# Blocks of v with 48 rows in place of 40 in an attention and feed-forward kernel

## The chip, the cores and the metric

The kernel runs on one core of one Trainium2 chip. The metric is the device time of one execution in microseconds, the median of several runs. The profile shows one further execution.

## What is computed

Three parts follow each other. First comes attention over 4 batches, 8 heads, 576 positions of 64 numbers, the sum of a coarse attention (q, k and v averaged over groups of four positions, its result repeated four times) and a local one, in which a position sees the seven positions around it. Then two feed-forward blocks work on the 2304 tokens of 512 numbers.

```python
out_d = sm_attn(q_d, k_d, v_d)                     # groups of four averaged
mask = np.abs(pos[:, None] - pos[None, :]) < 4
out_local = softmax(where(mask, scale * q @ k.T, -1e9)) @ v
x = (np.repeat(out_d, 4, axis=2) + out_local)      # 2304 tokens x 512
x = ((x @ w1) * (x @ w2) @ w3) @ w_out
h = x @ w_in
return (h * (1 / (1 + np.exp(-h)))) @ moe2_w_out
```

Inputs are drawn in 64-bit floats; the kernel loads q, k and v in 32 bits, and the weights as pairs of 32-bit words that VectorE and ScalarE turn into 32-bit floats. ("dec", "w_w", "st" and "lent" in the rows are tiles of this work.)

## The kernel before, in words

**Units.** Attention is cut into 16 units, each one batch and one pair of heads; one head of the pair takes partitions 0 to 63, the other 64 to 127. The names in the order list end in the unit's number: `sd`, `md`, `xd`, `rd`, `nd` are scores, maximum, exponentials and normalization of the coarse part, `s`, `mk`, `ml`, `x`, `rl`, `n` those of the local part, `td`, `cd`, `tl`, `cl` the transposes of the two sets of weights and ScalarE's copies of them, `od` and `ol` the products with v, `xf`, `xh`, `xo` their sum and its two halves for products in reduced precision.

**What a unit loads.** `Lq` (`load_qk`, L294) loads q and k, 128 rows of 4,632 bytes. `Lr` (`load_vr`, L307) loads v in groups of four, 80 rows of 4,096 bytes, for the pooled v (`pv0`, `pv1`; L478 and L485). `Lva` and `Lvb` (`load_vw`, L299) load v in blocks: for each window of 32 queries the 38 keys that it can see are laid out as 38 rows, with two rows of zeros to 40. `Lva` brings the even windows to partitions 0 to 39 (5,120 bytes a row), `Lvb` the odd windows to partitions 64 to 103 (two pieces of 2,048 bytes a row). The products of `ol` (`local_sums`, L504, matmuls on L516) read the 38 rows alone. The tile of the blocks, "vw", has one buffer: a unit's blocks are loaded when `ol` of the unit before is done. The tile of vr has one buffer too, freed by `pv1`. The arrays are laid out on the host in `kernel()`, outside the metric.

**Order.** The opening, up to the first products of x, is written out by hand as one list of names (`OPENING`): each name issues its instructions on their engines, and every engine runs its part in the order of the list. In it TensorE multiplies w3 with w_out (names `p...`, L628, tile "wp"), so that h @ w_out needs one product less later, while the first units' attention and the preparation of the weights go on in between; then the products of x with w1 and w2 begin (`ab...`, L668). The list has this order around the first loads:

```
Lwt000 Lwt001 Lwt002 Lq0 Lwo00 Lwo01 Lwt010 Lwt011 at00a d2t00a Lwo10 d1t00a Lwo11 at00b d3t00a
d2t00b d1t00b d3t00b Lva0 at00c d2t00c d1t00c d3t00c Lvb0 s0 pq0 Lr0 ao0a d2o0a sd0 z0 z1 mk0
ml0 Lq1 ...
```

After the opening a table (`SUMS`, `TURN`) says after how many steps of the products of x each unit's parts come; unit 15's products with v are done at some 304 us. What follows is feed-forward work in three stages (L1113, L1165, L1300), to the end.

**DMA.** SP alone issues DMAs. The issue of a load waits for what the tile's former users still do and for an earlier DMA, and SP works in order: a load that waits holds every DMA behind it. The opening's loads of weights (L228), of q and k (L296), of the blocks (L303) and of vr (L309) share this one queue.

Of the kernel before, what the change touches and what calls it, by code (L numbers as in the profile page):

```python
# [73 lines left out]
def tile_model(ctx: ExitStack, tc: tile.TileContext, qk, vw, vr, w12, w3t, wo, wb, out):  # L74
# [213 lines left out]
    A = {}  # L288
# [10 lines left out]
    def load_vw(u, par):  # L299
        if par == 0:  # L300
            A["vw", u] = att.tile([P, 2, 5, P], F32, tag="vw", name=f"vw{u}", bufs=1)
        n = 5 - par
        nc.sync.dma_start(  # L303
            A["vw", u][64 * par:64 * par + 40, :, :n, :], vw[u // 4, u % 4, par, :, :, :n, :]
        )

    def load_vr(u):  # L307
# [17 lines left out]
    def unit_ops(u):  # L325
# [249 lines left out]
        op("Lq" + U, lambda: load_qk(u))  # L575
        op("Lr" + U, lambda: load_vr(u))
        op("Lva" + U, lambda: load_vw(u, 0))
        op("Lvb" + U, lambda: load_vw(u, 1))
        op("pq" + U, lambda: pool_qk(u))

# [936 lines left out]
```

## Time and profile before

| | us |
|---|---|
| median of 3 runs | 808.66 |
| lowest and highest of them | 806.63, 809.44 |
| the profiled execution: its time | 808.23 |
| its span, first to last instruction | 806.4 |
| TensorE busy in the span | 791.4 (98%) |
| VectorE busy | 564.6 (70%) |
| ScalarE busy | 446.3 (55%) |
| GpSimd busy | 69.2 (9%) |

The rows further down are read like this. PE is TensorE, PEld its weight loads, DVE VectorE, ACT ScalarE, POOL GpSimd, SPq the queue of SP, which issues the DMAs. L303 is a line of the kernel. "vw<-vw" is a tile or array written from another; where both sides have one name, the left one is the tile on the chip. Times count from the start of the span. [...] A row of a wait names who waited, for whom, how long in total, how often, and the longest. A row of the chain has start, duration and what; a DMA there lasts from its issue to its landing. A row of a timeline has start, duration, engine, line, operation and count; in SP's it is the time of the issue, not of the transfer.

### The profile page before, as it was taken

How to read it: one execution, taken by the hardware profiler on the slowest of the kernel's cores; microseconds unless marked ns; L12 is line 12 of the kernel's file. 1: busy time of each engine (PE TensorE's matmuls, PEld its weight loads, DVE VectorE, ACT ScalarE, POOL GpSimd, SP SyncE). 2: the span in 40 equal slices, each digit the busy share in tenths (PEclk: the TensorE clock that was granted, in tenths of full speed). 3: DMA queues.
4: the chain of work that ended last, by engine and by line, in shares of the span. 5: the costliest groups of instructions: out<-in, count | busy, mean ns of one | idle time of the engine just before them, and what ended most of it. 6: DMA issues, size and time to landing. Idle time of an engine off the chain costs nothing.

```text
span 806.4 us, 19049 instructions
## 1 busy us (share of the span) xinstructions
PE 791.4 (98%) x7510; PEld 738.0 (92%) x7510; DVE 564.6 (70%) x870; ACT 446.3 (55%) x1136; POOL 69.2 (9%) x84
## 2 busy tenths in 40 slices
PE   9899999999999999999999999999999999999998
PEld 5455599889999999999999999999999999999998
DVE  7888885687698763746889567445466698777771
ACT  6588764745465452525457477547478545444441
POOL 3000100443243220000000000000000000000000
PEclk9999999999999999999999999999999999999999
DMA  9977864798898977225475553343887987777740
GB/s 301 365 230 224 261 204 139 238 295 280 269 306 278 297 248 246 51 51 229 154 296 174 194 182 118 137 148 112 235 263 239 287 207 184 193 191 185 194 133 27
DMA packets 132265, 168.68 MB, mean 209 GB/s; under 512 B 20176, under 2 KB 109776, under 8 KB 131792
## 3 DMA queue, kind: packets, MB, share of 16 engines
q1 hardware_dynamic: 132176, 167.46, 66.5%
q8 instruction: 59, 0.97, 0.5%
q14 instruction: 30, 0.25, 0.1%
HBM read 115.00 MB, written 52.43 MB: 208 GB/s over the span
## 4 chain that ended last, share of the span: by engine, by line
PE 85%; DMA 7%; DVE 3%; ACT 2%; SPq 1%; issue 1%; POOL 1%; DVEq 0%; ACTq 0%; POOLq 0%
PE ab L668 24%; PE yb L1113 11%; PE hx L1165 9%; PE ox L1300 8%; PE hy L1165 6%; PE oy L1300 5%; PE wp L628 4%; PE hv L1165 3%; PE hz L1165 3%; PE oz L1300 3%; PE ov L1300 2%; PE ol L516 2%; DMA A<-gd 2%; DMA qk<-qk 2%; PE od L494 1%; PE s L409 1%
## 5 line engine op out<-in xcount | busy, mean ns | idle before, releaser
L668 PE MATMUL ab<-x,w_wB 128*128 128x320 f32 (+1 forms) x768 | 108.9, 298 | 1.3 <-POOL x L546 0.9
L668 PE MATMUL ab<-x,w_wA 128*128 128x320 f32 (+1 forms) x768 | 107.0, 296 | 0.0
L668 PEld LDWEIGHTS ab<-x,w_wB 128*128 128x128 f32 x768 | 102.5, 188 | 2.9 <-issue 1.3
L668 PEld LDWEIGHTS ab<-x,w_wA 128*128 128x128 f32 x768 | 101.9, 188 | 0.5
L1113 PE MATMUL yb<-co,wy 128*128 128x384 f32 x504 | 87.5, 334 | 0.0
L1113 PEld LDWEIGHTS yb<-co,wy 128*128 128x128 f32 x504 | 87.3, 188 | 0.0
L1165 PE MATMUL hx<-yc,wc 128*128 128x384 f32 x432 | 83.0, 335 | 1.0 <-ACT u L1179 1.0
L1165 PEld LDWEIGHTS hx<-yc,wc 128*128 128x128 f32 x432 | 75.6, 188 | 1.3 <-ACT u L1179 1.3
L628 PE MATMUL wp<-w_wo,w_w 128*128 128x512 f32 x128 | 60.1, 602 | 0.2 <-DVE w_wo L198 0.2
L680 ACT COPY af<-ab 128x320 f32<-128x320 f32 (+1 forms) x64 | 25.4, 397 | 58.4 <-PE ab L668 55.8
L1165 PE MATMUL hy<-yc,wc 128*128 128x384 f32 x288 | 57.7, 335 | 0.0
L1300 PE MATMUL oy<-wo,S 128*128 128x256 f32 x432 | 54.8, 283 | 0.1
L1300 PE MATMUL ox<-wo,S 128*128 128x256 f32 x432 | 53.7, 280 | 0.4 <-ACT u2o L1313 0.4
L1300 PEld LDWEIGHTS oy<-wo,S 128*128 128x128 f32 x432 | 53.1, 192 | 0.3 <-ACT p5o L1311 0.3
L1300 PEld LDWEIGHTS ox<-wo,S 128*128 128x128 f32 x432 | 51.9, 190 | 0.7 <-ACT u2o L1313 0.6
L1149 ACT ACTIVATE c<-c 128x384 f32<-128x384 f32 x96 | 48.1, 525 | 5.9 <-DVE c L1079 5.0
L1165 PEld LDWEIGHTS hy<-yc,wc 128*128 128x128 f32 x288 | 50.7, 188 | 0.0
L686 DVE TENSOR_TENSOR cf<-ab,af 128x320 f32<-128x320 f32 (+1 forms) x64 | 28.9, 451 | 25.8 <-PE ab L668 10.9
L334 ACT ACTIVATE band<-band,sml 128x38 f32<-128x38 f32 x144 | 45.0, 321 | 2.1 <-DVE sml L425 2.1
L628 PEld LDWEIGHTS wp<-w_wo,w_w 128*128 128x128 f32 x128 | 22.4, 190 | 21.1 <-issue 18.7
L1171 ACT COPY p<-hx 128x384 f32<-128x384 f32 x24 | 11.5, 481 | 43.6 <-PE hx L1165 43.6
L980 DVE TENSOR_TENSOR co<-cb,co 128x768 fp32r<-128x768 f32 x32 | 29.3, 955 | 8.8 <-ACT co L979 8.1
(183 smaller groups left out, 1451.3 us busy)
## 6 DMA issues: line engine op xcount, KB each, us to landing
gd<-c SPq DMA_DIRECT2D x96, 192.0 KB
sw<-wb SPq DMA_DIRECT2D x32, 512.0 KB
qk<-qk SPq DMA_DIRECT2D x16, 579.0 KB
big<-gd SPq DMA_DIRECT2D x18, 512.0 KB
A<-gd SPq DMA_DIRECT2D x18, 512.0 KB
S<-gd SPq DMA_DIRECT2D x17, 512.0 KB
cb<-cd SPq DMA_DIRECT2D x10, 768.0 KB
st<-w SPq DMA_DIRECT2D x14, 512.0 KB
```

Source lines behind the costliest of these rows:

```text
L334: nc.scalar.activation(E[:, j, :], src[j], AF.Exp, bias=z[:, j:j + 1], scale=scale, accum_out=z[:, NQB + j:NQB + j + 1],)
L516: nc.tensor.matmul(acc[h][r, c0:c0 + QW], lhsT=v[k, sub, c, r], rhs=ET[k, c, q0:q0 + QW], start=True, stop=True,)
L628: nc.tensor.matmul(wp_ps[half, j], lhsT=w3v[:, k, j * P:(j + 1) * P], rhs=wov[:, k, :], start=(gp == 0 and k == 0), stop=(gp == 3 and k == 1),
L668: nc.tensor.matmul(acc[:, :N], lhsT=wv[:, i, w, kk, :], rhs=X[b, h, kk][:, j, :], start=(n == 0), stop=(n == 11),)
L680: mark(nc.scalar.copy(af, C.pop(("ab", b, h, m, 0))[:, :N]))
L686: nc.vector.tensor_tensor(out=cf, in0=C.pop(("ab", b, h, m, 1))[:, :N], in1=C.pop(("af", b, h, m)), op=ALU.mult)
L980: nc.vector.tensor_tensor(out=d[:, 1], in0=src, in1=d[:, 0].bitcast(F32), op=ALU.subtract)
L1113: nc.tensor.matmul(acc[e], lhsT=WY[o][:, a, 2 * g + k, c0:c0 + P], rhs=y[:, b, k, :], start=(n < 2 and (a, b) == (0, 0) and i in (0, 1, 2, ...
L1149: nc.scalar.activation(v, v, AF.Silu)
L1165: nc.tensor.matmul(acc, lhsT=WC[s][:, a, c, kt * P:(kt + 1) * P], rhs=y[:, b, kt, :], start=(n == 0 and i in (0, 1, 2, 4)), stop=(n == 5), ...
L1171: nc.scalar.copy(p1, X_)
L1300: nc.tensor.matmul(acc, lhsT=A[:, a, p * P:(p + 1) * P], rhs=B_[name, p // 4][:, b, p % 4, :], start=(p == 0 and q == 0 and name in begin) ...
```

## The change

Blocks of v are laid out with 48 rows, 38 of values and ten of zeros, and all 48 are loaded, to partitions 0 to 47 and 64 to 111. A load that ran on 10 DMA engines (four rows each) now runs on 16 (three rows each). The bytes of the two blocks of a unit go from 200 and 160 KB to 240 and 192. The products read the same 38 rows. No instruction is added, taken away or moved on any engine.

```diff
@@ load_vw
         n = 5 - par
         nc.sync.dma_start(
-            A["vw", u][64 * par:64 * par + 40, :, :n, :], vw[u // 4, u % 4, par, :, :, :n, :]
+            A["vw", u][64 * par:64 * par + 48, :, :n, :], vw[u // 4, u % 4, par, :, :, :n, :]
         )
@@ kernel
-    vw = np.zeros((B, H // 2, 2, 40, 2, 5, 2 * D), v.dtype)
+    vw = np.zeros((B, H // 2, 2, 48, 2, 5, 2 * D), v.dtype)
```

## Rows read from the trace of the kernel before

**Rows 1.** Busy time by stretch, around the opening and after it.

```profile
23.70:93.00 69.30, 69.22 (x888) 37.60 (x888) 60.08 (x105) 53.10 (x194) 0.00 (x0) 0.98 0.81 258
132.00:178.00 46.00, 43.31 (x794) 39.51 (x793) 34.40 (x77) 27.34 (x119) 19.68 (x19) 1.00 0.76 235
178.00:806.40 628.40, 622.39 (x5407) 615.05 (x5397) 424.41 (x613) 327.63 (x706) 39.26 (x42) 1.00 0.64 198
```

**Rows 2.** Waits of TensorE over the whole span.

```profile
PE s L409 <- DMA qk<-qk: 3.6, 1, 3.6
...
PE ab L668 <- POOL x L546: 0.9, 1, 0.9
...
PE tl L464 <- ACT ET L471: 0.6, 1, 0.6
...
PE tl L464 <- ACT EdT L453: 0.2, 1, 0.2
```

**Rows 3.** The chain that ended last, four pieces of its first 100 us.

```profile
3.08 7.68 DMA lent<-wo
...
10.78 12.84 DMA qk<-qk
...
72.57 7.76 DMA vr<-vr
...
95.47 0.29 PE tl L464
```

**Rows 4.** Timeline of SP's queue: the loads of unit 0's v, then qk1.

```profile
6.51 2.70 SPq L303 DMA_DIRECT2D vw<-vw  x2
9.49 0.33 SPq L309 DMA_DIRECT2D vr<-vr  x1
10.78 0.35 SPq L296 DMA_DIRECT2D qk<-qk  x1
```

**Rows 5.** Timeline of SP's queue in five short windows, 18.9 to 24 us.

```profile
19.05 0.33 SPq L228 DMA_DIRECT2D st<-w3t  x1
...
20.00 0.33 SPq L228 DMA_DIRECT2D st<-w3t  x1
...
21.47 0.33 SPq L228 DMA_DIRECT2D lent<-wo  x1
...
22.46 0.33 SPq L228 DMA_DIRECT2D lent<-wo  x1
...
23.64 0.33 SPq L228 DMA_DIRECT2D lent<-w3t  x1
```

**Rows 6.** Waits of SP's queue, 20.1 to 21.6 us.

```profile
SPq L228 <- DMA vw<-vw: 1.7, 2, 1.1
```

**Rows 7.** Busy time by stretch, before and during the loads of unit 0's v.

```profile
5.00:13.00 8.00, 7.38 (x102) 5.00 (x101) 7.79 (x17) 3.99 (x15) 2.53 (x7) 1.00 1.01 404
15.00:20.50 5.50, 5.09 (x17) 2.27 (x15) 3.21 (x7) 5.50 (x19) 0.00 (x0) 1.00 1.04 243
```

**Rows 8.** Timeline of SP's queue: the blocks of unit 3.

```profile
69.67 1.14 SPq L303 DMA_DIRECT2D vw<-vw  x2
```

**Rows 9.** Waits of VectorE, 62 to 96 us.

```profile
DVE vr L478 <- DMA vr<-vr: 1.1, 1, 1.1
DVE md L390 <- PE sd L380: 0.6, 1, 0.6
```

**Rows 10.** Busy time and granted clock, 24 to 28 us.

```profile
24.00:28.00 4.00, 4.00 (x81) 2.93 (x69) 3.40 (x4) 1.00 (x3) 0.00 (x0) 0.57 1.02 409
```

**Rows 11.** Timeline of TensorE: pooled scores of two units.

```profile
25.67 1.71 PE L380 MATMUL sd<-qkd 64*64 64x144 f32 x12
...
32.77 0.95 PE L380 MATMUL sd<-qkd 64*64 64x144 f32 x12
```

**Rows 12.** Busy time and DMA share while unit 2's first block is in transit.

```profile
57.30:57.80 0.50, 0.50 (x3) 0.22 (x2) 0.47 (x3) 0.50 (x1) 0.00 (x0) 1.00 0.53 215
```

## Prediction, made before the changed kernel was run

> **What bounds the kernel now.** I read the busy times by stretch first, then who waited for whom on TensorE, then the chain that ended last, and only then the DMA views of the places these point at. TensorE works 69.22 of the 69.30 us between 23.7 and 93, and all but 6 of the 628.4 us after 178 [rows 1]: it is the bound, and a faster load can only shorten one of its idle times. Its waits are few [rows 2]. The longest, 3.6 us, is for a load, that of q and k of unit 1 (qk1); 0.6 and 0.2 us go to transposes that wait for ScalarE, 0.9 to GpSimd. Between 132 and 178 it idles 2.7 us [rows 1], and no wait for a load is among them. So whatever the change gives must come ahead of 99 us, and is carried to the end from there.
>
> The chain says how the opening hangs together [rows 3]. Up to 23.62 us it is DMA alone: a load of wo issued at 3.08 lands at 10.76, which lets SP issue qk1 at 10.78, and that lands 12.84 us later and starts the local scores of unit 1. Then it is TensorE up to 61.9 us, VectorE up to 72.5, the load of vr of unit 3 (vr3) from 72.57 to 80.33, VectorE again, a weight load, ScalarE, and at 95.47 TensorE.
>
> **Where the blocks of v stand in it.** Each unit loads two, 40 rows of 5,120 and of 4,096 bytes: 200 and 160 KB. Those of unit 0 are issued from 6.51 us on (one merged row), then vr0 at 9.49 and qk1 at 10.78 [rows 4]. Eight DMAs are in flight: counted in SP's timeline, the issue at 10.78 is the eighth after that at 3.08 whose landing releases it, and so it goes on. Later issue times therefore tell the landings: SP issues at 19.05, 20.00, 21.47, 22.46 and 23.64 [rows 5], eight places after the second load of wo, the two blocks, vr0 and qk1, and the waits of 20.1 to 21.6 us are put down to vw [rows 6]. The pair costs 21.47 - 19.05 = **2.42 us** on the way to TensorE's longest wait. The stream is slow just there: 404 GB/s between 5 and 13 us, 243 between 15 and 20.5, both times with the DMA engines counted as fully busy [rows 7].
>
> **The change, part by part.**
> *The rows.* 40 rows over 10 engines are 4 rows an engine, 48 over 16 are 3. An engine that has part in the pair carries 27.6 KB in place of 36.9, a quarter less, and the six that had no part carry as much. A load has landed when its last engine is done; each landing above follows the one before, the two blocks among them, so I take the last engine to be one of the ten. Its pair: 0.75 x 2.42 = 1.82 us, **0.60 us less**. The ends: if the time goes by bytes moved and not by engines, it is 1.2 x 2.42 = 2.90, 0.48 us more. If the slow stretch comes from the uneven split alone, it lost 5.5 x (404 - 243) = 886 KB, 2.2 us at 404 GB/s, less 0.18 us for the 72 KB added: 2.0 us gained. I take 0.60: it is nearest to the issue times, which are read on this very path, while the other end would need the slow packets to have no other cause.
>
> *What that is worth.* qk1 lands 0.6 us earlier, and TensorE's 3.6 us shrink to 3.0. The later loads of the stream stand behind the same pair and move as much. TensorE then works without a gap up to 93 us, and waits 0.2 and 0.6 us for ScalarE, the second time at 95.47 [rows 2, 3]: that is what is late next. The chain that ends there began with TensorE's pooled scores, for which VectorE waited [rows 9], so the 0.6 us pass through it too.
>
> *Units 1, 2 and 4.* No wait of TensorE for their loads shows [rows 2]; in 23.7 to 93 it idles 0.08 us. I cost them at nothing: the cover is the product of w3 and wo that runs without a gap. Without it each pair would again give up to 0.6 us.
>
> *Unit 3.* Its pair is issued at 69.67 [rows 8], ahead of vr3 at 72.57, and vr3 is what VectorE waits 1.1 us for [rows 9]. A quarter of this pair is at most the 0.60 us above; at the full 404 GB/s, 25.2 an engine, 36.9 KB take 1.46 us, a quarter 0.37. I take 0.4, since fewer loads stand in this queue. It passes by VectorE and a weight load to ScalarE, and so into the 0.8 us that TensorE waits there, which also caps it.
>
> *Later pairs.* From unit 5 on they lie beside a TensorE that waits for no load [rows 2]: nothing. Their added bytes are 11 x 72 = 792 KB, 2.0 us of the stream at 404 GB/s, over some 180 us in which TensorE has its operands. Were that cover gone, each pair would cost 0.18 us.
>
> *Issue.* Two blocks issued together take SP 1.14 us [rows 8], where a load of 80 rows takes 0.33 and one of 128 rows 0.35 [rows 4]: the row count hardly counts. At worst a fifth is added, 0.2 us a pair, behind which SP waits for landings anyway. Rows 40 to 47 of each half are written and read by no product; instructions, order and waits of all engines stay the same.
>
> **The sum**, against the profiled execution's 808.23 us: -0.60 for qk1, -0.40 for vr3, 807.23. That execution lies 0.43 under the median of the runs shown, 808.66, so the forecast is **807.7 us**. A measurement of this kernel tells about 0.3%, 2.4 us, from no change (the three runs span 806.63 to 809.44), so I expect a gain too small to be told.
>
> [...] The row: the blocks move at 243 GB/s with every engine counted busy, 0.60 of the rate before [rows 7]. [...]
>
> **Rivals.**
> 1. *Slower: the blocks' time goes by their bytes.* [...] For it: the 243 GB/s at full share. Against: the last engine runs its pair when most are past theirs, so its own rows hold it. Price: +0.48 us on qk1 and +0.48 on vr3, 808.66 + 0.96 = **809.6 us**. It decides from the point at which the last engine's pair takes over 2.42 us.
> 2. *No change.* Another engine lands qk1 hardly earlier, or VectorE's work on the weights holds TensorE before 62 us, so that the 0.6 us turn into a wait there. For it: VectorE is busy 60.08 of those 69.30 us [rows 1]. Time: **808.7 us**.
> 3. *Faster: the clock stays up.* [...] The loss is 4.0 x 0.43 = 1.7 us. [...] Against it: 3.0 us are not much shorter than 3.6.
> 4. *The loads still go to ten engines.* Then each carries 4.8 rows and the pair takes 1.2 x 2.42 us: rival 1's time, 809.6. Against it: while one block alone is in transit the sixteen engines' share is 0.53 [rows 12], near ten sixteenths, so the number of engines does follow the rows, and 48 can be divided by 16.
>
> **How the numbers follow.** Chances: forecast 0.50, rival 1 0.18, rival 2 0.17, rival 3 0.12, rival 4 0.03. The range takes in rivals 3 and 1 with 0.3 us of scatter at either end: 805.7 to 809.9. What is left out, the gain of the whole 2.0 us together with the clock, or several pairs exposed at once, has under 0.2. Faster by over 0.3% means under 806.2: over half of rival 3 and some of the forecast's own scatter, 0.16. Slower by over 0.3% means over 811.1, which needs five exposed pairs at 0.48 us or causes I do not see: 0.07. Within: 0.77.
>
> **What would show it.** Right: the spacing of SP's issues that wait for the two blocks falls from 2.42 to about 1.8 us, TensorE's wait for qk from 3.6 to about 3.0, VectorE's for vr3 from 1.1 to about 0.7, and TensorE's transposes of 95.47 come near 94.5. Wrong: a spacing of 2.4 us or more (rivals 1 and 4); a shorter wait for qk with new waits of TensorE before 62 us (rival 2); a granted clock of 1.00 all through 24 to 28 us (rival 3). A time that moves with all these unchanged would mean that I read the wrong stretch.

## The result, and the profile after

The changed kernel took **812.53 us** (median of 20 runs, 807.40 to 818.71), the kernel before, beside it, 807.74 (20 runs, 804.08 to 813.17). The ratio is **1.0062, 95% interval 1.0043 to 1.0080**: slower by some 5 us, where 807.7 was forecast. The profiled execution of the changed kernel took 813.38 us, with a span of 811.6.

The first view shows how much work TensorE had in long stretches. In its rows, as in [rows 1, 7, 10, 12], stand the bounds, the length, the busy time of PE, PEld, DVE, ACT and POOL with the number of instructions, the clock granted to TensorE as a share of full speed, the mean busy share of the sixteen DMA engines, and the GB/s that they moved. The kernel before:

```profile
0.00:178.00 178.00, 169.00 (x2122) 122.92 (x2123) 140.18 (x258) 118.72 (x430) 29.90 (x42) 0.99 0.79 250
...
178.00:290.00 112.00, 111.63 (x1769) 106.07 (x1760) 87.26 (x183) 61.62 (x258) 35.98 (x39) 1.00 0.89 291
```

The changed kernel, with the stretches of [rows 1, 7] as well:

```profile
15.00:20.50 5.50, 5.49 (x18) 2.43 (x16) 3.34 (x8) 4.97 (x19) 0.00 (x0) 1.00 1.05 179
...
23.70:93.00 69.30, 68.15 (x886) 37.71 (x887) 60.05 (x105) 52.92 (x192) 0.00 (x0) 0.98 0.88 269
132.00:178.00 46.00, 41.82 (x735) 38.12 (x735) 34.91 (x74) 26.68 (x117) 19.06 (x18) 1.00 0.74 218
...
0.00:178.00 178.00, 165.73 (x2060) 120.85 (x2061) 139.86 (x255) 118.31 (x428) 29.53 (x41) 0.99 0.81 249
...
178.00:290.00 112.00, 109.84 (x1715) 103.78 (x1714) 86.21 (x181) 61.02 (x256) 34.39 (x37) 1.00 0.90 294
```

TensorE is busy 3.27 us less by 178 us and 1.79 us less from there to 290: 5.06 of the 5.2 us by which this span is longer. The stream at the blocks of unit 0 moves 179 GB/s in place of 243 [rows 7], the engines' share being full in both (1.05 and 1.04), and TensorE is no longer without a gap from 23.7 to 93 us.

TensorE's waits over the span, after:

```profile
PE s L409 <- DMA qk<-qk: 4.4, 2, 3.7
PE ol L516 <- ACT Ed L334: 2.2, 2, 1.6
PE ab L668 <- issue: 2.1, 1, 2.1
...
PE ab L668 <- POOL x L546: 1.2, 1, 1.2
...
PE tl L464 <- ACT ET L471: 0.3, 1, 0.3
```

Beside [rows 2], the wait for qk1 went from 3.6 to 3.7 us (the longest of its row; the other 0.7 us is a wait for q and k of unit 0, at 8 us); the transposes' waits shrank from 0.6 and 0.2 to 0.3; two waits are new in size, for ScalarE's weights `Ed` and one that the view puts down to nothing ("issue"). Here they stand in the timeline of TensorE, after:

```profile
55.96 1.25 PE L516 MATMUL ol<-ET,vw 38*64 38x32 f32 x68 [0.65 <-DVE vr L478]
...
95.92 0.29 PE L464 MATMUL tl<-ident,band 128*38 128x128 f32 x1 [0.30 <-ACT ET L471]
...
155.43 1.25 PE L516 MATMUL ol<-ET,vw 38*64 38x32 f32 x68 [1.64 <-ACT Ed L334]
...
289.75 2.32 PE L668 MATMUL ab<-x,w_wB 128*128 128x256 f32 x18 [2.10 <-issue]
```

Two of them go back to loads. In the chain that ended last the vr of unit 1 (issued at 41.28) stands behind the first, and behind that at 155.43 a load of weights (tile sw) that lands at 148.55; VectorE decodes it, and is late with the maxima on which ScalarE's `Ed` depends. The chain, after, with vr3 in the second row, which was issued 2.05 us later than before and landed 1.1 us later (81.41 for 80.33 us [rows 3]):

```profile
41.28 13.88 DMA vr<-vr
...
74.62 6.79 DMA vr<-vr
...
139.74 8.81 DMA sw<-wb
```

How long VectorE waited for that load is the clearest row of the later loss. Before, 136 to 156 us:

```profile
DVE sw L192 <- DMA sw<-wb: 1.3, 1, 1.3
```

After, the same stretch, with the two waits of 62 to 96 us that answer to [rows 9]:

```profile
DVE sw L192 <- DMA sw<-wb: 4.0, 1, 4.0
...
DVE vr L478 <- DMA vr<-vr: 1.4, 1, 1.4
DVE md L390 <- PE sd L380: 1.0, 1, 1.0
```

Put side by side product by product, TensorE in this execution is 0.5 us late at 23.7, 1.4 at 55.8, 0.5 again at 95.5 and 0.2 at 143.9; it loses 2.1 us between there and 154 and 1.7 at 287. So in this execution the opening's loss was largely taken up again, and most of what stayed came from 143 us on, where the prediction costed nothing.

### The profile page after: what moved, and what is told of

Its sections match the earlier page's. It is cut to its first block, busy times and chain, and to the rows that moved or that the text cites. A ratio compares the mean times of both kernels' runs of the same rounds, so it can differ in the third digit from the quotient of the medians.

```text
span 811.6 us, 19049 instructions
## 1 busy us (share of the span) xinstructions
PE 791.2 (97%) x7510; PEld 738.2 (91%) x7510; DVE 565.2 (70%) x870; ACT 446.7 (55%) x1136; POOL 69.1 (9%) x84
## 4 chain that ended last, share of the span: by engine, by line
PE 82%; DMA 11%; DVE 3%; ACT 1%; issue 1%; SPq 1%; POOL 1%; DVEq 0%; ACTq 0%; POOLq 0%
PE ab L668 23%; PE yb L1113 11%; PE hx L1165 9%; PE ox L1300 8%; PE hy L1165 6%; PE oy L1300 5%; PE hv L1165 3%; PE hz L1165 3%; PE oz L1300 3%; DMA vr<-vr 3%; PE ov L1300 2%; DMA A<-gd 2%; PE ol L516 2%; DMA qk<-qk 2%; DMA st<-wo 1%; DMA lent<-wo 1%
```

## The experiments

Each ratio is to the kernel before, run beside it on the same chip, with its 95% interval. Four kernels went together each time, two the last time. All compute the full result.

**First set: layout, early loads, late loads.** The array keeps 48 rows; how many are loaded is `r`: 40 for all units; 48 for units 0 to 3 alone; 48 from unit 4 on; and the change as it is, once more. The theories were that the loss arises in the opening (A) or at the later pairs (B).

```diff
-            A["vw", u][64 * par:64 * par + 40, :, :n, :], vw[u // 4, u % 4, par, :, :, :n, :]
+            A["vw", u][64 * par:64 * par + r, :, :n, :], vw[u // 4, u % 4, par, :r, :, :n, :]
...
-    vw = np.zeros((B, H // 2, 2, 40, 2, 5, 2 * D), v.dtype)
+    vw = np.zeros((B, H // 2, 2, 48, 2, 5, 2 * D), v.dtype)
```

Layout alone, `r = 40`:

> The array of blocks has 48 rows, but 40 of them are loaded, over ten engines as before. If the loss comes from what the loads do (all theories below), the time is that of before: ratio 1.000, within 0.002. If the rows' new place in memory were the cause, 1.006.

`r = 48 if u < 4 else 40`:

> 48 rows for units 0 to 3 alone, 40 for the others. Theory A (the blocks' time goes by their bytes at half of the tile's partitions, and the opening, whose DMA stream is full, lands later): nearly the whole loss, ratio 1.004 to 1.006, with the loads of 40 to 60 us 3 us or more later. Theory B (the opening takes the delay back; the loss comes from the pairs from unit 4 on, which now hold up weights and the program's own loads on six engines that were free of blocks): 1.000 to 1.001.

`r = 40 if u < 4 else 48`:

> 40 rows for units 0 to 3, 48 from unit 4 on. Theory A: 1.000 to 1.002. Theory B: 1.004 to 1.006, the loss in steps of 1 to 2 us at single places between 120 and 300 us, where TensorE waits for ScalarE's exponentials or for nothing that the profile shows.

The change again:

> The change as it is, for a second profile. The ratio should be 1.006 again (1.004 to 1.008). Theory A and B both have the opening's loads late once more; by theory B the steps between 120 and 300 us come again, though not at the same places if it is a matter of which transfer meets which; if all the difference were scatter of the single execution, no step over 0.5 us would come there.

| kernel | median us | ratio | interval |
|---|---|---|---|
| layout alone | 809.52 | 1.0038 | 1.0012 to 1.0063 |
| first units | 810.31 | 1.0045 | 1.0025 to 1.0065 |
| later units | 809.65 | 1.0044 | 1.0021 to 1.0066 |
| the change | 814.93 | 1.0099 | 1.0067 to 1.0131 |

The change came out above the 1.004 to 1.008 expected of it. Neither half of the loads holds the loss, and a layout whose loads move the same bytes through the same ten engines costs, within the intervals, as much as either. The second profile of the change repeats the wait for sw (4.1 us on VectorE), and shows what followed it. Two stretches of it:

```profile
15.00:20.50 5.50, 5.50 (x18) 2.65 (x17) 4.55 (x10) 5.50 (x24) 0.00 (x0) 1.00 1.05 237
...
157.00:161.00 4.00, 4.00 (x42) 3.80 (x35) 2.24 (x6) 3.73 (x20) 2.29 (x3) 0.57 0.79 259
```

TensorE waited 1.8 us for ScalarE at 154, and the clock granted after it is 0.57 on average from 157 to 161, where the kernel before has 1.00: 4.0 x 0.43 = 1.7 us more. After the 1.64 us of the first profile it did not fall.

**Second set: is it the array, the bytes or the engines?** The kernel before with an edit that changes no instruction; the 40-row layout with a longer array; 39 and 44 rows loaded from the 48-row layout. Where a load's data landed could be read from the trace's events: 40 rows use ten engines (ten landings a load), 39 thirteen, 44 eleven, 48 sixteen.

```diff
-    A = {}
+    A = dict()
```

> The kernel before, unchanged, for a second profile and as a measure of what comparing a kernel with itself gives. Ratio 1.000, within 0.002. If what the layout alone cost (1.0038) was scatter between programs, this one may lie as far from 1; if the place of the arrays in memory costs, it lies at 1.000.

```diff
-    vw = np.zeros((B, H // 2, 2, 40, 2, 5, 2 * D), v.dtype)
+    vw = np.zeros((B + 1, H // 2, 2, 40, 2, 5, 2 * D), v.dtype)
...
-            vw[:, :, i % 2, :KW, sub, i // 2] = vp[:, :, k0:k0 + KW]
+            vw[:B, :, i % 2, :KW, sub, i // 2] = vp[:, :, k0:k0 + KW]
```

> Blocks of 40 rows, laid out and loaded as before, in an array a quarter longer, so that what lies behind it in memory moves and nothing else changes. Theory C (the place of the arrays costs): 1.003 to 1.005. Theories A and B (the loads of 48 rows cost, and the layout alone only seemed to): 1.000, within 0.002.

39 rows (`r = 39` in the first set's diff):

> The longer layout, 39 rows loaded: 13 engines with three rows each, a fortieth fewer bytes than before. Theory A (cost by bytes at half of the partitions): as the layout alone, 1.002 to 1.004, and the median engine lands qk1 at 21.1 to 21.5 us, as with ten engines. Theory E (cost by the engines that take part, since each of them then stands in the slow blocks): as the change, 1.005 to 1.008, median landing of qk1 at 22.2 us or later. By the prediction's step (fewer rows on the last engine): 0.999 or less.

44 rows (`r = 44`):

> The longer layout, 44 rows loaded: 11 engines with four rows each, a tenth more bytes than before. Theory A: half of the difference between the layout alone and the change, 1.005 to 1.007, TensorE's wait for qk1 a quarter us longer. Theory E: as the layout alone, 1.002 to 1.004.

| kernel | median us | ratio | interval |
|---|---|---|---|
| same kernel | 807.15 | 1.0001 | 0.9981 to 1.0021 |
| longer array, 40 rows | 808.81 | 1.0027 | 1.0007 to 1.0047 |
| 39 rows, 13 engines | 811.88 | 1.0069 | 1.0046 to 1.0092 |
| 44 rows, 11 engines | 810.85 | 1.0050 | 1.0029 to 1.0071 |

An edit that changes no instruction moves nothing. A longer array of which no load knows measures 0.27% slower. And 39 rows, fewer bytes than before on more engines, have the highest ratio of the four, in an interval that overlaps that of 44 rows: that speaks against the added bytes alone. For the number of engines that take part (theory E) the sign that was named did not come: half of the engines had landed qk1 by 20.96 us, as with ten engines (20.8 to 21.7 in ten profiles), where 22.2 or later was expected. And both kernels had the layout's own loss in them. So neither theory is shown by them, and that a block's place in half of the tile's partitions has a part in it, as theory A supposes, was tested by no run.

The 39 rows show something else. SP's issues that wait for the load of wo, the second block and qk1, in that kernel:

```profile
18.55 0.33 SPq L228 DMA_DIRECT2D st<-w3t  x1
...
19.40 0.43 SPq L228 DMA_DIRECT2D lent<-wo  x1
...
21.52 0.33 SPq L228 DMA_DIRECT2D lent<-w3t  x1
```

With 39 rows over thirteen engines, three each by count, the pair took 19.40 - 18.55 = 0.85 us in place of 2.42, qk1 landed 2.1 us earlier than before [rows 5], and TensorE, compared product by product with the kernel before, is 2.8 us ahead at 99 us. At 178 us it is 2.3 us behind. So in this execution the prediction's step came true in full, and its gain was not carried to the end.

**Third set: unit 6, and the place of the array.** The sw load of 139 us is issued in the time of unit 6's blocks. If they delay it (theory D), unit 6 at 40 rows should give the wait back. The other two give vw the last place among the inputs, with 48 and with 40 rows loaded.

```diff
+        r = 40 if u == 6 else 48
...
```

> 48 rows for all units but unit 6, whose blocks are issued at 142 us, while the weight load (sw, issued at about 139.5) that the next decoding waits for is under way. Theory D (at 11 and more engines the blocks of unit 6 hold back the last piece of that load, from 7 us to over 8, and ScalarE's exponentials and TensorE's products with v wait for it): the load lands in under 7.5 us, TensorE's wait of its products with v for ScalarE falls under 0.6 us, and the time is 1.5 to 2.5 us below the change's, ratio 1.004 to 1.006 where the change has 1.006 to 1.010. If other pairs cost (or scatter), as the change: the load at 8 us or more, ratio 1.006 to 1.010.

`r = 48 if u == 6 else 40`:

> 48 rows for unit 6 alone, in the longer layout. Theory D: the load lands 8 to 9 us after its issue, TensorE's products with v wait 1.5 us or more for ScalarE, and the ratio is 0.0015 to 0.0025 above that of the layout alone (1.0038): 1.005 to 1.0065. If unit 6 does not matter: 1.003 to 1.004 and a load of 7 us.

```diff
-        "qk": qk, "vw": vw, "vr": vr, "w12": w12, "w3t": w3t,
-        "wo": inputs["moe_w_out"], "wb": wb,
+        "qk": qk, "vr": vr, "w12": w12, "w3t": w3t,
+        "wo": inputs["moe_w_out"], "wb": wb, "vw": vw,
...
+    args.insert(1, args.pop())
...
```

> The change, with the array of the blocks declared as the last input, so that its length moves no other input. Theory C (a part of the loss, 1.003 to 1.004, is the place of the arrays in memory): 1.003 to 1.006, clearly under the change's. If the place costs nothing: 1.006 to 1.010.

The same with `r = 40`:

> The longer layout with 40 rows loaded, the array declared as the last input. Theory C: 1.000, within 0.0015. If the longer stride between blocks costs by itself, or the order of the inputs does not set their place: 1.003 to 1.004.

| kernel | median us | ratio | interval |
|---|---|---|---|
| all but unit 6 | 810.72 | 1.0029 | 1.0008 to 1.0051 |
| unit 6 alone | 811.88 | 1.0048 | 1.0020 to 1.0077 |
| the change, array last | 810.32 | 1.0027 | 1.0001 to 1.0053 |
| layout alone, array last | 807.40 | 0.9998 | 0.9976 to 1.0019 |

Theory D fell. With unit 6 at 40 rows VectorE's wait for sw, 136 to 156 us, is as long as with the change:

```profile
DVE sw L192 <- DMA sw<-wb: 4.5, 1, 4.5
```

and the load behind it takes, in that kernel's chain:

```profile
141.69 8.79 DMA sw<-wb
```

With unit 6 alone at 48 rows VectorE's wait is 3.8 us, hardly more than the 3.5 that the longer array has with 40 rows throughout. It is these waits that speak against theory D and not the time: 1.0029 lies under the range of either theory.

The last row of the table seemed to settle the layout: with the array in another place its loss is gone. So the next set ran both placements on one further chip.

**Fourth set: both placements together.**

The change:

> The change, on one chip with the next three. If place in memory and rows loaded add up (0.3% each): ratio 1.005 to 1.008.

Layout alone:

> The longer layout with 40 rows loaded, array in its old place. If the place of the arrays behind it costs 0.3%: 1.002 to 1.005, and 0.002 to 0.004 under the change. If what the earlier run showed was scatter: 1.000.

The change, array last:

> 48 rows loaded, array last. The loads' own share: 1.002 to 1.004, 0.002 to 0.004 over the layout with the array last; the mean landing over the sixteen engines from the second load of wo to qk1 takes 5.3 us or more, where ten engines took 4.6 to 5.1. If the loads cost nothing: 1.000.

Layout alone, array last:

> 40 rows loaded, array last. If place and loads are the two causes, neither is at work here: 1.000, within 0.002.

| kernel | median us | ratio | interval |
|---|---|---|---|
| the change | 811.16 | 1.0055 | 1.0029 to 1.0082 |
| layout alone | 812.15 | 1.0061 | 1.0040 to 1.0082 |
| the change, array last | 809.54 | 1.0040 | 1.0018 to 1.0062 |
| layout alone, array last | 809.93 | 1.0041 | 1.0024 to 1.0058 |

A miss: the layout alone with the array last had been 0.9998 and is now 1.0041, intervals that don't meet. And in this set the loads add nothing to the layout, in either place. The mean landing named for the change with the array last, 5.3 us or more, came out at 5.05. From one set to another the same kernel moves by some 0.4% against the kernel before (the change: 1.0062, 1.0099, 1.0055), more than the intervals within a set say. To tell the loads from the layout, the layout had to go.

**Fifth set: the loads alone.** The blocks stand 40 rows apart as before, eight rows of zeros are put behind the whole array, and a load of 48 rows takes the next block's first eight with it. The partner has the same array and loads 40.

```diff
+        r0 = 40 * (2 * u + par)
...
-            A["vw", u][64 * par:64 * par + 40, :, :n, :], vw[u // 4, u % 4, par, :, :, :n, :]
+            A["vw", u][64 * par:64 * par + 48, :, :n, :], vw[r0:r0 + 48, :, :n, :]
...
+    vw = np.concatenate([vw.reshape(-1, 2, 5, 2 * D), np.zeros((8, 2, 5, 2 * D), v.dtype)])
```

> The old layout of 40 rows a block, with eight rows of zeros behind the last one; 48 rows are loaded, the last eight of them being the first of the next block, which no product reads. So the loads are those of the change and the array is as long as before but for 41 KB. If the loads cost (sixteen engines, a fifth more bytes): 1.002 to 1.004. If the longer layout was all of it: 1.000 to 1.001.

> The same array with its eight rows more, 40 rows loaded: as before in all but 41 KB of length. If only the layout's growth by a fifth matters, or the loads: 1.000, within 0.002. If any other array gives a time up to 0.4% off (place in memory by chance of each program): anywhere from 0.998 to 1.004.

| kernel | median us | ratio | interval |
|---|---|---|---|
| 48 rows, blocks 40 apart | 812.24 | **1.0060** | 1.0030 to 1.0089 |
| 40 rows, blocks 40 apart | 807.38 | 0.9998 | 0.9971 to 1.0024 |

The number of rows loaded is all that differs between the two, and the loss between them is as large as the change's. Their line numbers from L302 on are one higher than in the kernel before. Stretches of the kernel with 48 rows:

```profile
15.00:20.50 5.50, 5.45 (x18) 2.40 (x16) 3.58 (x8) 5.50 (x20) 0.00 (x0) 1.00 1.03 239
...
0.00:178.00 178.00, 165.29 (x2049) 119.65 (x2050) 136.79 (x254) 117.40 (x426) 27.84 (x41) 0.99 0.80 246
```

and with 40:

```profile
15.00:20.50 5.50, 5.50 (x19) 2.67 (x17) 4.11 (x9) 5.50 (x23) 0.00 (x0) 1.00 1.03 255
...
0.00:178.00 178.00, 168.96 (x2115) 123.22 (x2117) 139.81 (x258) 118.66 (x430) 30.22 (x42) 0.99 0.77 250
```

VectorE's waits of 62 to 96 and of 136 to 156 us, with 48 rows:

```profile
DVE st L192 <- DMA st<-w: 3.0, 2, 2.4
DVE vr L479 <- DMA vr<-vr: 2.9, 1, 2.9
...
DVE sw L192 <- DMA sw<-wb: 3.4, 1, 3.4
```

and with 40:

```profile
DVE vr L479 <- DMA vr<-vr: 1.3, 1, 1.3
...
DVE st L192 <- DMA st<-w: 0.4, 1, 0.4
...
DVE sw L192 <- DMA sw<-wb: 1.6, 1, 1.6
```

The view of the tile vr between 68 and 86 us, with 48 rows, gives its load's time from issue to landing:

```profile
DMA to landing us min/median/max: 9.3/9.3/9.3
```

And the timeline of TensorE has, with 48 rows, a wait that the partner has not:

```profile
93.69 0.52 PE L435 MATMUL td<-ident,Ed 128*72 128x128 f32 x3 [2.03 <-DVE xf L530]
```

TensorE is busy 3.67 us less by 178 us. The load vr3 takes 9.3 us (before it was 7.76 [rows 3]), VectorE waits 1.6 us longer for it and 2.6 longer for weights, and the transposes `td` wait 2.03 us for VectorE; at the sw load VectorE waits 1.8 us longer again. None of these are loads of blocks: they are what stands in the queue beside and behind them. Compared product by product, TensorE falls 4.3 us behind the partner between 60 and 96 us, regains 1.2 by 150, and loses 1.0 at 153; the granted clock of both executions is 0.998. So the two main places of the loss, in this execution, are those at which VectorE waits for a load.

In this pair the loss comes with the loads alone, and is more than the 0.2 to 0.4% expected of them. But it is one pair, and its 0.6% is not far above the 0.4% by which one kernel moved between sets. Five pairs differ in nothing but the rows loaded. In the order of the tables, the ratio with 48 rows is higher than that with 40 by 0.0061 (first set), 0.0029 (third, array last), -0.0006 and -0.0001 (fourth), and 0.0062 here, on average 0.0029. That the loads cost time is likely by this; how much of the change's 0.6% they are is not settled.

**What holds over all profiles.** Twenty profiles are on record, one of the kernel before, one of the change and one for each run of the five sets. VectorE's wait for vr3 separates them: 0.4 to 1.3 us in the ten with ten engines at unit 3, 1.4 to 2.9 in the eight with sixteen. Its wait for sw does not. It is 2.6 to 4.1 us in the six with 48 rows throughout, but 1.3 to 3.5 in the eight with 40 throughout: 1.3, in the kernel before, is the shortest of all twenty, the longer layouts and the longer array have 1.9 to 3.5, and the kernel with the edit that changes no instruction has

```profile
DVE sw L192 <- DMA sw<-wb: 2.5, 1, 2.5
```

TensorE's loss at 153 us follows this wait in all twenty, whatever is loaded: at most 0.1 us up to a wait of 2.6, and 0.4 to 2.3 us from 3.2 on. On average over those eight and six, TensorE stands, beside the profiled kernel before, 0.6 us ahead and 0.2 behind at 99 us, 0.2 and 0.4 behind at 150, 0.9 and 2.5 at 178, and 1.3 and 3.5 at the end. So nearly all of the average difference, 2.2 us, comes after 150 us and not in the opening. But it is less than the spread of the single profiles, which at the end is 4.6 us among the eight and 7.2 among the six, so a row of one profile shows where a loss can come, not what the change costs there.

## Why the prediction was wrong

**The step that failed** is the term "I take the last engine to be one of the ten. Its pair: 0.75 x 2.42 = 1.82 us, **0.60 us less**", as a gain of qk1. The pair did shorten, and that bought nothing. The issues of SP that answer to [rows 5], after:

```profile
20.01 0.33 SPq L228 DMA_DIRECT2D st<-w3t  x1
...
20.83 0.33 SPq L228 DMA_DIRECT2D st<-w3t  x1
...
21.68 0.33 SPq L228 DMA_DIRECT2D lent<-wo  x1
...
22.95 0.33 SPq L228 DMA_DIRECT2D lent<-wo  x1
...
24.17 0.33 SPq L228 DMA_DIRECT2D lent<-w3t  x1
```

The pair now takes 21.68 - 20.01 = 1.67 us, less than the 1.82 forecast. But the load of wo ahead of it lands almost 1 us later (20.01 for 19.05), and vr0 and qk1 behind it take 24.17 - 21.68 = 2.49 us for 23.64 - 21.47 = 2.17. The sum, 4.16 for 4.59, gained 0.43 and the start lost 0.96, so qk1 came 0.5 us later, and TensorE's wait for it, forecast at 3.0 us, was 3.7. I had divided one stretch of a shared stream and left its neighbours as they were.

The 2.42 itself was one draw. The same spacing in ten profiled executions whose unit 0 uses ten engines runs from 1.24 to 2.76 us, mean 2.1, and in eight with sixteen engines from 1.7 to 2.2, mean 1.9; the issue released by qk1's landing comes at 23.2 us on average with ten (21.9 to 24.8) and at 23.6 with sixteen (22.9 to 25.1). On average, then, the pair gains 0.2 us and not 0.60, the load of wo ahead of it lands 0.7 later (19.3 for 18.6), and vr0 and qk1 take 2.4 either way. That the changed kernel's profile met the 1.82 was luck: a term of 0.60 us was read from one difference of issue times that scatters by 1.5.

**"The later loads of the stream stand behind the same pair and move as much"**, forward: the opposite. Averaged over all sixteen engines, in the trace's events, unit 0's stretch from the second load of wo to qk1 takes 4.6 to 5.1 us with ten engines and 5.05 to 6.4 with sixteen; at unit 1, from the load of w3 ahead of its blocks to the next behind them, 4.1 to 4.85 against 5.2 to 6.1. The last engine hardly gains and the average loses about 1 us a pair. The averages fit six engines that had no part in a block, ran ahead to the loads behind it, and now queue at it too; which engine did what is not shown. Slower, by what the blocks cost the loads beside them, was the direction of **rival 1**, and its evidence, 243 GB/s at full share, was in hand; the point from which it was to decide, a last engine whose pair takes over 2.42 us, did not come (2.2 at most). In 15 to 20.5 us the ten kernels with ten engines at unit 0 move 243 to 279 GB/s, mean 262, the eight with sixteen 179 to 260, mean 233.

**Unit 3: -0.40 us.** VectorE's wait for vr3 went from 1.1 to 1.4 us in the changed kernel, and to 2.9 in the pair that isolates the loads (1.3 there with 40 rows). The transposes forecast near 94.5 came at 95.92 after 95.47 [rows 3]. The sign was wrong, for the same reason: from the load of weights ahead of unit 3's blocks to vr3 the average engine takes 2.6 to 3.0 us with ten engines there and 3.5 to 3.8 with sixteen.

**"Units 1, 2 and 4. I cost them at nothing"**: the cover was only as thick as one execution showed. In the changed kernel vr of unit 1 takes 13.88 us from issue to landing, and TensorE waits 0.65 us for what VectorE makes of it.

**"Later pairs ... nothing"** was the dearest omission of the profiled execution, and the price that rival 1 had wrong as well: it stopped at qk1 and vr3 (+0.96, 809.6 us). TensorE waits for no load after 100 us, that was read rightly [rows 2]; but VectorE does. Its wait for sw was 1.3 us before and is 4.0, 4.1 and 2.6 in three executions of the change and 3.4 in the loads alone, and TensorE's loss at 153 us follows it (1.9, 2.2, 0.1 and 1.0 us). What makes just this load late is not shown: unit 6's own blocks are not it (theory D), and VectorE waits up to 3.5 us for it with 40 rows.

**"And is carried to the end from there"** was not borne out either: the 39 rows were 2.8 us ahead at 99 us and ended 1.0069, and the changed kernel, 0.5 behind at 95.5, ended 5 us behind.

**The clock (rival 3)** has a part in it, with the wrong sign. In the kernel before the granted clock stands at 0.50 from 24.5 to 27.5 us, after TensorE's wait of 3.6 us for qk1, and is 0.57 on average from 24 to 28, so that the stretch costs 4.0 x 0.43 = 1.7 us [rows 10]; twelve products of pooled scores take 1.71 us there and 0.95 later [rows 11]. The lower end of the range counts those 1.7 us as gained if the wait is 3.0 us; no run shows that gain. In the opening it fell in sixteen of the twenty profiles, whose longest wait for qk was 2.1 to 4.8 us, and stayed up in four, where it was 1.4 to 2.8: that leans rival 3's way, though the two ranges overlap. After the change's wait of 3.7 us it fell as before, later. Stretches after the change:

```profile
24.00:26.00 2.00, 1.80 (x78) 1.40 (x80) 1.92 (x3) 0.40 (x2) 0.00 (x0) 0.79 1.03 414
26.00:30.00 4.00, 4.00 (x24) 2.63 (x25) 3.19 (x6) 2.08 (x9) 0.00 (x0) 0.68 1.02 407
```

That is 2.0 x 0.21 + 4.0 x 0.32 = 1.7 us, no more than before; in the repeat a second stretch came at 157 us (first set). That longer waits bring more such stretches is the author's estimate, and fits the runs' clocks. Over 20 runs of the change the mean granted clock is 0.9956, over the 29 runs of the kernel before in the first set 0.9987. The difference is 0.0031 x 807 = 2.5 us, half of the loss. The other half shows where no clock was lost: at 1.000 the change took 808.7 us on average (2 runs), the kernel before 806.2 (14 runs). This is arithmetic on the runs, no experiment.

**Rival 2** (a wait of VectorE in place of the gain) describes a part of it. **Rival 4** is out: the data of a 48-row load landed on sixteen engines. **The range** was too narrow at the upper end, since five exposed places at half a microsecond were given 0.07 and the layout was costed at nothing at all.

**What stays open.** How much of the 0.6% is the loads', since five pairs give from nothing to all of it. Why a longer layout, with the loads unchanged, cost 0.4 to 0.6% in three measurements and nothing in one; why loads and layout do not add up (1.0055 and 1.0061 in one set, 1.0099 and 1.0038 in another); and the 2.10 us at 287 us in the changed kernel's profile, for which it shows no releaser (0.37 before the same product in the kernel before, 0.7 in the repeat of the change, but 1.28 in the kernel with the edit that changes no instruction and 1.74 in the layout alone with the array last: so it is no mark of the change). That the array's place in memory matters is the obvious guess, but the placement runs contradict each other. No kernel tried beat the one before.

## What to carry to other kernels

Giving a small load more DMA engines did not help here, where every engine was counted busy already (a share of 1.04 at the blocks of unit 0 [rows 7]), and the six with no part in the blocks had the next loads to carry, as far as the landings tell. Price such a change on the loads beside and behind it, and on every engine that waits for a load, not on TensorE's waits alone: in the repeat of the change the late sw load reached TensorE through VectorE and ScalarE (VectorE waited 4.1 us for the load, TensorE 1.8 for ScalarE), and the clock granted after it was 0.57 from 157 to 161 us. And before a term of half a microsecond is taken from one profiled execution, look how the same quantity scatters, in a second profile of the same kernel if there is one.

## What the runs showed that was not expected

- Loads of 48 rows, in place of 40 of the same array, made the whole kernel 0.6% slower in the last set (1.0060 against 0.9998) and 0.3% on average over five pairs, though their extra bytes are 16 x 72 KB in 169 MB moved.
- With 39 rows qk1 landed 2.1 us earlier than before, and the kernel was slower all the same.
- 39 rows on thirteen engines, with fewer bytes than 40 on ten, gave 1.0069 (1.0046 to 1.0092), with the longer layout.
- Laying out an input with unused rows, or making its array a quarter longer, moved the time by up to 0.6% with the same loads (1.0038, 1.0061; 1.0027; with the array last 0.9998 and 1.0041).
- The runs of one kernel differ in good part by the granted clock: the kernel before took 805.6 to 806.2 us on average at 1.000 in the five sets, and the two runs of the changed kernel at 0.989, in its first measurement, took 818.6.
